# The first loads of a fused attention and feed-forward kernel, issued in another order and on other queues

## The chip, the cores and the metric

The kernel runs on one core of one Trainium2 chip. The metric is device time in microseconds (us) of the whole execution. A core has TensorE (PE in the profile; PEld is its weight load), VectorE (DVE), ScalarE (ACT), GpSimd (POOL) and SyncE (SP). SP and ACT can both issue DMA transfers; a "q" after an engine's name (SPq, ACTq) means its sequencer, which issues and waits. Times inside a profile count from the start of the span; the device time is about 1.3 us longer than the span.

The granted clock is the share of PE's full clock that the profile records. Where a trace has such records, they begin when the clock is first raised, which the mean granted clock does not count as a loss. In the profile of before the warm-up matmuls of 512 columns are 0.427 us apart. A trace that holds no clock record at all also says 1.0, so there I go by the pace of the matmuls.

## The reference, cut to what matters

```python
# x: [1, 2048, 640]; wqkv: [640, 1920]; w_phi: [32, 20, 20]; gate_w: [640]
q, k, v = split_heads(x @ wqkv)                       # 32 heads of 20
phi_k = concat(softmax(k @ w_phi), softmax(-(k @ w_phi)))    # the same for q
kv, z = phi_k.T @ v, phi_k.sum(over tokens)
a = ((phi_q @ kv) / (phi_q @ z + 1e-6)) @ wo
b = (gelu(x @ w_gate) * (x @ w_up)) @ w_down
out = sigmoid((x * gate_w).sum(-1)) * a + (1 - ...) * b
```

The tokens come in 16 tiles of 128. The change touches only the first 30 us: how x and wqkv arrive, and the first products of v.

## The kernel before

Two parts of the kernel matter. The first issues the loads. `xtok` holds the first four tiles of x in token order, and PE transposes them itself. `xT` holds x transposed; its other twelve tiles are transposed by the DMA on the way in (`dma_start_transpose`), as are wk and wq. `w3[:, kt, 0:640]` is the kt-th block of 128 rows of the v weights; I call these five loads "the rows of wv". `sc.dma(queue, ..., reads, writes)` makes the issuing engine wait for whatever the named keys need.

```python
xload("sp", 0)                      # tiles 0 and 1 of x
xload("act", 2)                     # tiles 2 and 3, beside it
sc.dma("act", ... wphi ...)
for kt in range(KD):                # KD = 5
    sc.dma("sp", ... self.w3[:, kt, 0:D] <- w3[:, kt, 2*D:3*D] ..., writes=[("wv", kt)])
sc.dma("act", ... gate row ...)
xturn(4, 2)                         # x of tiles 4 and 5, transposing load on SP
wload(self.wkT, D, "wkT")           # wk, transposing load
xturn(6, 2)
wload(self.wqT, 0, "wqT")
xturn(8, 4); xturn(12, 4)
# ... all other weights, on SP
```

The second is what TensorE does first. `vs(t, kt)` multiplies tile t by row block kt of wv. PE takes its instructions in order, so when the data of one are missing, everything behind it waits. A bank is a part of PSUM (ps in the profile), where PE's products lie until ACT or DVE evacuates them, that is, copies them out. To fold a row block of wk or wq is to multiply it by w_phi; `pq` is a product of x with the folded wq; the gram is phi_k.T @ v.

```python
warm(7)                             # 7 matmuls of zeros, to raise PE's clock
xt(0, 6, "d"); xt(1, 7, "a"); xt(2, 2, "d"); xt(3, 3, "a")  # transpose; evacuate on DVE / ACT
for kt in range(4):
    for t in range(4): vs(t, kt)    # (written out in the kernel)
self.blockdiag(); self.gate_column(6)
# ... vs(t, 4), v of tiles 4, 5; fold wk blocks 0, 1; v of tile 6; fold wk 2, 3, 4; v of tile 7;
# ... then k of tile 0, fold wq, ..., pq(0,1), pq(0,0), pq(0,3)
```

The softmax here doesn't subtract the row's maximum and nothing guards it: scores larger than these inputs give would overflow.

## Time and profile before

| | before |
|---|---|
| time, 6 runs | 288.41 us median, 287.72 to 289.37 |
| PE busy | 281.2 of 286.9 us (98%) |
| first real work on PE | 4.29 us |
| rows of wv landed | 4.96, 6.43, 6.86, 7.30, 7.80 us |
| x of tiles 6 and 7 landed | 14.76 us |
| wq landed | 19.97 us |

The landings are read from the semaphore updates in the trace. The page of the kernel before shows the busy share of each engine in its first part:

```profile
PE 281.2 (98%) x3017; PEld 185.5 (65%) x3032; DVE 174.7 (61%) x353; ACT 105.0 (37%) x199; POOL 5.3 (2%) x36
```

PE has almost no room, so a change of the loads can win or lose only where PE waits. Here is PE's timeline of the first 15 us in the kernel before. The columns are start, length, engine, line, operation, output and inputs, and count; the brackets hold idle time and who ended it.

```profile
4.29 1.29 PE L291 MATMUL ps<-ident,xtok 128*128 128x128 bf16 x20
5.42 4.72 PE L364 MATMUL ps<-w,xT 128*128 128x480 bf16 x32
9.98 0.22 PE L314 MATMUL ps<-ident,gz 128*128 128x128 bf16 x1
10.03 1.25 PE L364 MATMUL ps<-w,xT 128*128 128x480 bf16 x8
11.33 2.66 PE L352 MATMUL ps<-w,xT 128*128 128x512 bf16 x19
13.84 0.79 PE L332 MATMUL ps<-BD,wkT 128*128 128x140 bf16 x12
14.80 1.04 PE L352 MATMUL ps<-w,xT 128*128 128x512 bf16 x4 [0.18 <-DMA xT<-in_A_x_dram]
```

The 32 first v matmuls (L364) follow one another from 5.42 to 10 us. The view of waits, limited to PE and the first 30 us, lists every wait of PE above 0.15 us in the kernel before (total, times, longest):

```profile
PE ps L541 <- DVE zero L537: 1.2, 1, 1.2
PE ps L352 <- ACT Eq L519: 0.3, 1, 0.3
PE ps L352 <- DMA xT<-in_A_x_dram: 0.2, 1, 0.2
```

### The profile page before, as it was taken

To read this page: it belongs to the slowest core of one execution; us is meant where nothing else is said; L and a number is where in the kernel's file an instruction comes from. 1 tells how busy PE (TensorE), PEld (TensorE's weight loads), DVE (VectorE), ACT (ScalarE), POOL (GpSimd) and SP (SyncE) were. 2 spreads that over 40 slices of the span, in tenths; PEclk is the share of its full clock that TensorE was granted. 3 is DMA by queue.
4 is the path that set the end of the run, shared out by engine and by line. 5 is a ranking of instruction groups with operands and counts; after the bars stand their busy time and mean duration, and the time that the engine had idled before them with its cause. 6 is when DMAs were issued, how large, how long until landed. Compare 5 with 4: busy or idle time off the path is not lost.

```text
span 286.9 us, 7006 instructions
## 1 busy us (share of the span) xinstructions
PE 281.2 (98%) x3017; PEld 185.5 (65%) x3032; DVE 174.7 (61%) x353; ACT 105.0 (37%) x199; POOL 5.3 (2%) x36
## 2 busy tenths in 40 slices
PE   8999999999999999999999999999999999999996
PEld 3666689999994444444444444445777777777785
DVE  3248999999977553567242334225883883883801
ACT  3367887677663322322323223221112112112111
POOL 7000000000000000000000000000000000000000
PEclk9999999999999999999999999999999999999999
DMA  8999995000002000011000000000232333422221
GB/s 226 206 187 247 367 367 174 0 2 2 2 0 48 0 0 0 3 24 23 2 0 0 0 2 0 0 2 0 25 94 62 35 48 92 49 49 85 56 72 48
DMA packets 36937, 18.67 MB, mean 65 GB/s; under 512 B 28970, under 2 KB 36394, under 8 KB 36906
## 3 DMA queue, kind: packets, MB, share of 16 engines
q1 hardware_dynamic: 36096, 17.86, 26.1%
q8 instruction: 24, 0.39, 0.6%
q10 hardware_dynamic: 810, 0.35, 0.5%
q14 instruction: 7, 0.06, 0.1%
HBM read 9.04 MB, written 2.62 MB: 41 GB/s over the span
## 4 chain that ended last, share of the span: by engine, by line
PE 93%; SPq 3%; DMA 2%; ACT 1%; issue 1%; ACTq 0%
PE ps L352 60%; PE ps L714 28%; PE ps L658 2%; DMA xT<-in_A_x_dram 2%; PE ps L450 2%; SPq L221 2%; PE ps L332 1%; SPq L234 1%; SPq L225 1%; ACT Ek L414 0%; ACT Eq L519 0%; SPq L217 0%; ACT outsb L727 0%; ACT gcol L417 0%; ACTq L42 0%
## 5 line engine op out<-in xcount | busy, mean ns | idle before, releaser
L352 PE MATMUL ps<-xT,wg_sb 128*128 128x512 bf16 (+1 forms) x265 | 63.8, 379 | 0.4 <-issue 0.2
L352 PE MATMUL ps<-xT,wu_sb 128*128 128x512 bf16 (+1 forms) x263 | 63.3, 379 | 0.5 <-DVE hT L632 0.2
L630 ACT ACTIVATE gl<-ps 128x512 bf16<-128x512 f32 x52 | 30.9, 596 | 73.1 <-PE ps L352 68.7
L632 DVE TENSOR_TENSOR hT<-ps,gl 128x512 bf16<-128x512 f32 x39 | 26.7, 690 | 38.6 <-PE ps L352 38.5
L714 PE MATMUL ps<-wd_sb,hT 64*128 64x320 bf16 x648 | 49.5, 296 | 0.0
L352 PEld LDWEIGHTS ps<-xT,wu_sb 128*128 128x128 bf16 (+1 forms) x270 | 26.5, 99 | 29.8 <-DVE hT L632 0.5
L352 PEld LDWEIGHTS ps<-xT,wg_sb 128*128 128x128 bf16 (+1 forms) x270 | 26.2, 99 | 29.0 <-ACT gl L630 0.2
L352 PE MATMUL ps<-w,xT 128*64 128x512 bf16 (+6 forms) x398 | 41.6, 325 | 0.4 <-DMA xT<-in_A_x_dram 0.2
L727 ACT ACTIVATE outsb<-ps,Gm 128x320 bf16<-128x320 f32 (+2 forms) x31 | 14.5, 515 | 72.4 <-PE ps L714 72.4
L352 PEld LDWEIGHTS ps<-w,xT 128*64 128x64 bf16 (+1 forms) x400 | 35.8, 107 | 5.1 <-DMA xT<-in_A_x_dram 0.4
L714 PEld LDWEIGHTS ps<-wd_sb,hT 64*128 64x128 bf16 x648 | 31.0, 94 | 12.1 <-issue 0.4
L714 PE MATMUL ps<-wo_sb,goT 64*128 64x320 bf16 (+2 forms) x340 | 27.8, 288 | 0.0
L352 PE MATMUL ps<-xT,wq 128*64 128x512 bf16 (+1 forms) x184 | 26.1, 381 | 0.4 <-ACT Eq L519 0.3
L434 DVE TENSOR_TENSOR Ek<-Ek,Dk 128x640 bf16<-128x640 bf16 x32 | 25.0, 822 | 0.6
L685 DVE TENSOR_TENSOR O<-ps,RH 128x640 bf16<-128x640 f32 x32 | 24.8, 816 | 0.0
L425 DVE TENSOR_REDUCE Dk<-Ek 128x64 f32<-128x1280 bf16 x16 | 23.7, 1479 | 0.1
L519 ACT ACTIVATE Eq<-ps 128x512 bf16<-128x512 f32 x40 | 21.7, 605 | 1.1 <-PE ps L352 0.8
L414 ACT ACTIVATE Ek<-ps 128x640 bf16<-128x640 f32 x32 | 20.7, 703 | 3.6 <-PE ps L352 3.6
L632 DVE TENSOR_TENSOR xT<-ps,gl 128x512 bf16<-128x512 f32 x13 | 9.0, 691 | 18.2 <-PE ps L352 18.2
L714 PEld LDWEIGHTS ps<-wo_sb,goT 64*128 64x128 bf16 x340 | 16.1, 94 | 5.4
L352 PEld LDWEIGHTS ps<-xT,wq 128*64 128x64 bf16 (+1 forms) x185 | 15.3, 109 | 3.4 <-ACT Eq L519 0.8
L714 PE MATMUL ps<-wd_sb,xT 64*128 64x320 bf16 (+2 forms) x270 | 16.7, 269 | 0.0
(69 smaller groups left out, 173.2 us busy)
## 6 DMA issues: line engine op xcount, KB each, us to landing
out_dram<-outsb SPq DMA_DIRECT2D x7, 320.0 KB, 2.3
wd_sb<-in_B_w_down_dram SPq DMA_DIRECT2D x1, 2080.0 KB, 14.3
wg_sb<-in_B_w_gate_dram SPq DMA_DIRECT2D x1, 1120.0 KB, 5.7
wu_sb<-in_B_w_up_dram SPq DMA_DIRECT2D x1, 1120.0 KB, 8.2
wg_sb<-in_B_w_gate_dram SPq DMA_DIRECT2D x1, 960.0 KB, 9.8
wu_sb<-in_B_w_up_dram SPq DMA_DIRECT2D x1, 960.0 KB, 10.4
w<-in_A_wqkv_dram SPq DMA_DIRECT2D x5, 160.0 KB, 4.7
wo_sb<-in_A_wo_dram SPq DMA_DIRECT2D x1, 800.0 KB, 9.7
```

The costliest lines, as they stand in the source:

```text
L221: sc.dma("sp", lambda e: e.dma_start_transpose(T[:, :, :], self.wqkv[:, c0:c0 + D]), writes=[key])
L352: self.sc.op("pe", lambda e: e.matmul(self.ps[a:z, bank * 512 + c0:bank * 512 + c0 + n], lhs[:, a:z], rhs, start=first, stop=fin), reads=r ...
L414: self.sc.op("act", lambda e, s=s, scale=scale: e.activation(self.Ek[:, se, s, :], self.ps[:, o:o + self.D], AF.Exp, scale=scale), reads=[ ...
L425: sc.op("dve", lambda e: e.tensor_reduce(self.Dk[:, se, 0, :].rearrange("p (s h) -> p s h", h=H), self.Ek[:, se, :, :].rearrange("p s (h d ...
L434: sc.op("dve", lambda e, v=v, r=r: e.tensor_tensor(v, v, r, ALU.mult), reads=[("Rk", se)], writes=[("Ek", se, s)])
L450: sc.op("pe", lambda e: e.matmul(self.ps[a:a + 64, b * 512 + c:b * 512 + c + 2 * nf], va[:, lo:lo + 64], self.Ek[:, se, :, f0:f0 + nf], st ...
L519: sc.op("act", lambda e, s=s, scale=scale: e.activation(self.Eq[:, s, i, b * self.BT:(b + 1) * self.BT], self.bank(bank), AF.Exp, scale=sc ...
L630: sc.op("act", lambda e: e.activation(self.gl[:, slot, :], self.bank(banks[0]), AF.Gelu_apprx_tanh), reads=[("ps", banks[0])], writes=[("g ...
L632: sc.op("dve", lambda e: e.tensor_tensor(hT, self.bank(banks[1]), self.gl[:, slot, :], ALU.mult), reads=[("ps", banks[1]), ("gl", slot)], ...
L685: dve(lambda e, o=o, f=f, s=s: e.tensor_tensor(o, V[s][:, :, :, 0:DH], f, ALU.mult), rb + [key(6 + s)], [("O", s, sl)], guard=old)
L714: sc.op("pe", lambda e: e.matmul(self.bank(bk, w), lhs, rhs, start=opens and x == 0, stop=end and not opens, skip_group_check=True), reads ...
L727: sc.op("act", lambda e: e.activation(dst, self.bank(bk, w), AF.Copy, scale=g), reads=rd, writes=wr)
```

## The change

Its intent is to start PE's real work sooner and to remove those waits. The first two tiles of x get the DMA engines to themselves. Two of the five rows of wv go to ACT's queue, so that SP comes to its transposing loads sooner; they wait for x so as not to compete with it. w_phi and the gate row, needed late, go last. wk is turned in two parts, so that x of tiles 6 and 7 need not wait behind all of it. The warm-up reads a constant in place of a memset buffer, and pq(0,3) gets a free bank.

```diff
+        def vload(q, a, z):
+            sc.dma(q, lambda e: e.dma_start(self.w3[:, a:z, 0:D], w3[:, a:z, 2 * D:3 * D]),
+                   reads=[("xtok", 0)] if q == "act" else (), writes=[("wv", kt) for kt in range(a, z)])
...
-        xload("sp", 0)
-        xload("act", 2)
-        sc.dma("act", ... wphi ...)
+        sc.op("act", ... a first Exp, to load its table early ...)
+        for j in (0, 2):
+            xload("sp", j)
         for kt in range(KD):
-            sc.dma("sp", ... w3[:, kt, 0:D] ...)
-        sc.dma("act", ... gate row ...)
+            vload("act" if kt % 2 else "sp", kt, kt + 1)
         xturn(4, 2)
-        wload(self.wkT, D, "wkT")
+        wload(self.wkT, D, "wkT", 0, 2)
         xturn(6, 2)
-        wload(self.wqT, 0, "wqT")
+        wload(self.wkT, D, "wkT", 2, 5)
+        wload(self.wqT, 0, "wqT", 0, 5)
...
-        warm(7)
+        for n in (512, 512, 512, 512, 512, 512, 128):
+            ... matmul of the constant 1.0, n columns ...
...
-        xt(3, 3, "a")
+        xt(3, 3, "d")
+        sc.dma("act", ... wphi ...)
+        sc.dma("act", ... gate row ...)
...
-        self.pq(0, 3, 3)
+        self.pq(0, 3, 3, 0)
```

(Left out: the keys of wk and wq become one per row block, so that folding a block waits for its part only.)

More of the change, by code (lines that the diff above doesn't have):

```diff
@@ L156, in alloc @@
         self.ident = T("ident", [P, P], BF16)
-        self.zero = T("zero", [P, 512], BF16)
         self.gz = T("gz", [P, P], BF16)
@@ L218, in xload, with wload @@
                    writes=[("xtok", j), ("xtok", j + 1)])
-        def wload(T, c0, key):
-            sc.dma("sp", lambda e: e.dma_start_transpose(T[:, :, :], self.wqkv[:, c0:c0 + D]), writes=[key])
+        def vload(q, a, z):
+            sc.dma(q, lambda e: e.dma_start(self.w3[:, a:z, 0:D], w3[:, a:z, 2 * D:3 * D]),
+                   reads=[("xtok", 0)] if q == "act" else (), writes=[("wv", kt) for kt in range(a, z)])
+        def wload(T, c0, key, a, z):
+            sc.dma("sp", lambda e: e.dma_start_transpose(T[:, :, a * P:z * P], self.wqkv[a * P:z * P, c0:c0 + D]),
+                   writes=[(key, k) for k in range(a, z)])
         def xturn(t, n):
@@ L227, in loads @@
         sc.op("pool", lambda e: e.memset(self.gz[:, :], 0.0), writes=["gz"])
-        xload("sp", 0)
-        xload("act", 2)
-        sc.dma("act", lambda e: e.dma_start(
-            self.wphi_sb[:, :, :], self.wphi.rearrange("h d f -> (h d) f").rearrange("(i p) f -> p i f", p=P)),
-            writes=["wphi"])
+        sc.op("act", lambda e: e.activation(self.gtmp[:, 0:1], self.nc.const_aps.tensor(1.0, [P, 1], BF16), AF.Exp),
+              writes=["gtmp"])
+        for j in (0, 2):
+            xload("sp", j)
         for kt in range(KD):
-            sc.dma("sp", lambda e: e.dma_start(self.w3[:, kt, 0:D], w3[:, kt, 2 * D:3 * D]), writes=[("wv", kt)])
-        sc.dma("act", lambda e: e.dma_start(self.gz[0:KD, :], self.gw.rearrange("(k p) -> k p", p=P)), writes=["gz"])
+            vload("act" if kt % 2 else "sp", kt, kt + 1)
         xturn(4, 2)
-        wload(self.wkT, D, "wkT")
+        wload(self.wkT, D, "wkT", 0, 2)
         xturn(6, 2)
-        wload(self.wqT, 0, "wqT")
+        wload(self.wkT, D, "wkT", 2, 5)
+        wload(self.wqT, 0, "wqT", 0, 5)
         xturn(8, 4)
@@ L334, in fold @@
                     start=first, stop=fin, skip_group_check=True),
-                    reads=["w%sT" % which, ("BD", i)], writes=[("ps", b)], signal=fin)
+                    reads=[("w%sT" % which, kt), ("BD", i)], writes=[("ps", b)], signal=fin)
         src = self.pair(banks)
@@ L510, in kv_mask, with pq @@
                 self.kvk[i, r].append(("KV", i, r, g))
-    def pq(self, b, i, n):
+    def pq(self, b, i, n, bank=None):
         sc = self.sc
-        bank = 6 + n % 2
+        bank = 6 + n % 2 if bank is None else bank
         for kt in range(self.KD):
@@ L536, in attention_state @@
         sc = self.sc
-        sc.op("dve", lambda e: e.memset(self.zero[:, :], 0.0), writes=["zero"])
-        def warm(n):
-            for i in range(n):
-                sc.op("pe", lambda e: e.matmul(self.bank(0), self.zero[:, 0:P], self.zero[:, :], start=True, stop=True),
-                      reads=["zero"], writes=[("ps", 0)])
+        ones = self.nc.const_aps.tensor(1.0, [P, 512], BF16)
+        for n in (512, 512, 512, 512, 512, 512, 128):
+            sc.op("pe", lambda e: e.matmul(self.bank(0, n), ones[:, 0:P], ones[:, 0:n], start=True, stop=True),
+                  writes=[("ps", 0)])
         vs, ve, xt = self.v_step, self.v_first_evac, self.x_transpose
-        warm(7)
         xt(0, 6, "d")
@@ L547, in attention_state @@
         xt(2, 2, "d")
-        xt(3, 3, "a")
+        xt(3, 3, "d")
+        sc.dma("act", lambda e: e.dma_start(
+            self.wphi_sb[:, :, :], self.wphi.rearrange("h d f -> (h d) f").rearrange("(i p) f -> p i f", p=P)),
+            writes=["wphi"])
+        sc.dma("act", lambda e: e.dma_start(self.gz[0:self.KD, :], self.gw.rearrange("(k p) -> k p", p=P)), writes=["gz"])
         for t in range(4):
@@ L651, in num @@
         DB, DH = self.DB, self.DH
-        old = [("xtok", k) for k in range(4)] + ["wkT", "wqT"]
+        old = [("xtok", k) for k in range(4)] + [(w, k) for w in ("wkT", "wqT") for k in range(self.KD)]
         w = self.HB * DB
```

## The prediction

> All times are microseconds from the span's start in the profile of before, unless said otherwise.
>
> **What bounds the kernel.** TensorE. The page's first part has PE busy 281.2 of 286.9 us (98%); the chain of waits gives PE 93%, and from 30 us to the end it is PE alone but for short pieces. The change removes no matmul of that part, so all it can win is what PE loses in the first 30 us.
>
> **Where PE loses time (timeline and single instructions):**
> 1. Both x loads land together, at 4.2 and 4.4: two queues share the same engines. The Trainium skill, "DMA: Bandwidth & Descriptors", section "Issuing engines are not separate DMA queues", says DMAs interleave whoever issues them; the trace agrees: packets of both run side by side from 1.8 to 4.0. Real PE work starts at 4.28, after 7 warm-up matmuls of 0.427 us pitch that began only at 1.24, behind the memset of zero on DVE.
> 2. The first v steps wait 0.2 us for evacuations on ACT (0.70 us each, against 0.49 on DVE).
> 3. PE waits about 0.34 us before 14.80 for xT of tiles 6 and 7, queued behind the whole wkT (landing 14.75).
> 4. About 0.1 us before 20.01 for wqT (landing 19.97).
> 5. About 0.3 us before 28.34 for the Eq evacuation in the bank that pq(0,3) reuses.
>
> **What the change does.**
> - x in turn on one queue: the first half, 320 KB, should land about 3.3 (packets from 1.8 at the 300 GB/s of before, plus 0.45 us of receipt read from the trace), the second still about 4.3. Warm-up starts about 0.4 us earlier and ends about 3.5; transposes of tiles 0 and 1 then fill 3.5 to 4.3, wholly or partly at half clock. Tiles 2 and 3 follow, with DVE evacuations. I expect the first v round to end 0.3 to 0.6 us earlier (before: 6.69).
> - wv rows 1 and 3 on ACT's queue wait for x; they should land about 5.5 to 6, before they are needed. SP's queue loses two issues of 0.47 us and gains one: all transposes start about 0.45 us earlier.
> - wkT in two parts lets tiles 6 and 7 land near 12.5: loss 3 goes.
> - wphi and gate rows late: landings near 8 to 8.5, needed at about 9.6 (gate). No wait expected, margin about 1 us.
> - wqT lands about 0.45 us earlier, 19.5. PE would want it at about 19.2, so this load decides: the gain here is about 0.45, not PE's 0.8.
> - pq(0,3) into bank 0 removes loss 5: another 0.3 us.
> After that PE has hardly a wait. DVE's k_norm chain runs without a break from 25.3 to 79 but shifts too, so the gain should survive.
>
> **Predicted:** 287.75 us, 0.8 less than 288.56 (0.3%), range 286.9 to 288.6. Chances: faster by over 2% 0.01, within 2% 0.98, slower by over 2% 0.01.
>
> **What would show it right:** first transposes on PE near 3.5; no idle on PE before the matmuls that read tile 6; no wait for ACT before pq(0,3); wqT landing near 19.5 and ending a wait on PE.
>
> **What would make it wrong:** the clock released later than the 4.3 us of before, so that the early work runs at half rate (the Trainium skill, "TensorE: Matmul & The Clock Gate", Part 1: the window runs free; 0.427 us per 512 columns shows the half rate here); wphi or gate row landing after 9.6, stalling PE; split transposes taking longer in sum, delaying wqT.

## The result, and the profile after

The changed kernel took 292.96 us in the median of 6 runs, 292.49 to 293.94 in its five fast ones. The sixth, 334.62 us, ran at 0.85 of PE's clock for nearly the whole span and is set aside; no other run did that. The ratio of the changed kernel's fast runs to those of before is 1.0159 (95% interval 1.0133 to 1.0186). Ratios here are the mean time of one kernel's fast runs over that of the other's in the same rounds, so they are not quite the ratio of the medians. The kernel became 4.6 us slower (mean of the fast runs, 293.03 against 288.44) where I had forecast 0.8 us faster.

The profile taken with that result was the slow run, so I ran the same kernel again. That run (called e0_again below) is the profile after. PE is busy as long as before, in a longer span:

```profile
PE 281.1 (97%) x3017; PEld 185.8 (64%) x3032; DVE 174.9 (61%) x353; ACT 104.5 (36%) x199; POOL 5.3 (2%) x36
```

The timeline of PE in this run, from the transposes of x (L294) on:

```profile
3.76 1.71 PE L294 MATMUL ps<-ident,xtok 128*128 128x128 bf16 x20
5.66 1.25 PE L367 MATMUL ps<-w,xT 128*128 128x480 bf16 x8 [0.19 <-DMA w<-in_A_wqkv_dram]
9.74 3.45 PE L367 MATMUL ps<-w,xT 128*128 128x480 bf16 x24 [2.84 <-DMA w<-in_A_wqkv_dram]
13.04 0.22 PE L317 MATMUL ps<-ident,gz 128*128 128x128 bf16 x1
```

PE does begin 0.5 us sooner, as intended. But after the first 8 v matmuls it stands still until 9.74 us. The waits of PE over the first 30 us in this run:

```profile
PE ps L367 <- DMA w<-in_A_wqkv_dram: 3.0, 2, 2.8
PE ps L542 <- PEq L834: 0.8, 1, 0.8
```

The three small waits of before are gone or shorter, and one of 3 us is new. The chain of waits of this run, in order of time, says which DMA it was:

```profile
3.73 5.96 DMA w<-in_A_wqkv_dram
9.70 0.05 issue
9.74 3.45 PE ps L367 x24
```

The load issued at 3.73 us is row block 1 of wv, the first of the two on ACT's queue. It took 5.96 us for 160 KB. The list of DMA issues shows the two queues side by side (last column: median us from issue to landing). Before:

```profile
w<-in_A_wqkv_dram SPq DMA_DIRECT2D x5, 160.0 KB, 4.7
```

and in the run after:

```profile
w<-in_A_wqkv_dram SPq DMA_DIRECT2D x3, 160.0 KB, 3.8
w<-in_A_wqkv_dram ACTq DMA_DIRECT2D x2, 160.0 KB, 6.1
```

So the three on SP came faster than before and the two on ACT much later than was needed: row blocks 1 and 3 landed at 9.70 and 10.35 us, while PE wanted block 1 at about 6.7.

That is a pause of 3 us; the kernel lost 4.6. A second loss shows in the granted clock, which is listed for each run. Here are all fast runs of the changed kernel, from both rounds of measurement, in order of clock:

| mean granted clock | times (us) |
|---|---|
| 1.0 | 289.92 |
| 0.994 | 291.87, 292.49, 292.81, 292.85, 293.07 |
| 0.988 | 293.34, 293.73, 293.94 |

One window of 3.413 us at half clock in 291.6 us gives 1 - 0.5 * 3.413 / 291.6 = 0.994, and two give 0.988. The medians of the rows are 289.92, 292.81 and 293.73 us, so 3.8 us lie between no window and two. The steps are uneven, 2.9 us for the first window and 0.9 for the second, and the first row is a single run, so this table does not give the price of one window. By arithmetic, a window of 3.413 us at half clock that PE could fill would cost 1.7 us.

### The profile page after: what moved, and what is told of

Same layout as the page of the kernel before. It is cut to its first block, busy times and chain, and to the rows that moved or that the text cites. A ratio compares the mean times of both kernels' runs of the same rounds, so it can differ in the third digit from the quotient of the medians.

```text
span 333.3 us, 7008 instructions
## 1 busy us (share of the span) xinstructions
PE 324.9 (97%) x3017; PEld 201.5 (60%) x3032; DVE 175.9 (53%) x353; ACT 105.6 (32%) x199; POOL 5.3 (2%) x36
## 4 chain that ended last, share of the span: by engine, by line
PE 94%; DMA 3%; DVE 1%; issue 0%; ACT 0%
PE ps L355 60%; PE ps L718 28%; DMA w<-in_A_wqkv_dram 2%; PE ps L662 2%; PE ps L367 2%; PE ps L453 2%; PE ps L335 1%; DMA xtok<-in_A_x_dram 1%; DVE O L689 0%; DVE hT L636 0%; DVE RH L678 0%; ACT outsb L731 0%; DVE RH L683 0%; DVE RH L684 0%; DVE RH L682 0%
## 5 line engine op out<-in xcount | busy, mean ns | idle before, releaser
L355 PE MATMUL ps<-xT,wg_sb 128*128 128x512 bf16 (+1 forms) x265 | 73.1, 422 | 0.5 <-issue 0.2
L355 PE MATMUL ps<-xT,wu_sb 128*128 128x512 bf16 (+1 forms) x263 | 72.7, 423 | 0.6
L718 PE MATMUL ps<-wd_sb,hT 64*128 64x320 bf16 x648 | 56.4, 324 | 0.0
L355 PEld LDWEIGHTS ps<-xT,wu_sb 128*128 128x128 bf16 (+1 forms) x270 | 28.6, 107 | 36.7
L355 PE MATMUL ps<-w,xT 128*64 128x512 bf16 (+6 forms) x398 | 48.1, 359 | 0.2
L355 PEld LDWEIGHTS ps<-w,xT 128*64 128x64 bf16 (+1 forms) x400 | 38.1, 116 | 8.9
L718 PEld LDWEIGHTS ps<-wd_sb,hT 64*128 64x128 bf16 x648 | 33.6, 101 | 16.1 <-issue 0.5
L718 PE MATMUL ps<-wo_sb,goT 64*128 64x320 bf16 (+2 forms) x340 | 31.3, 315 | 0.0
L355 PE MATMUL ps<-xT,wq 128*64 128x512 bf16 (+1 forms) x184 | 30.0, 420 | 0.1
L678 DVE RECIPROCAL RH<-ps 128x32 f32<-128x32 f32 x16 | 5.7, 358 | 25.6 <-PE ps L662 25.0
## 6 DMA issues: line engine op xcount, KB each, us to landing
wo_sb<-in_A_wo_dram SPq DMA_DIRECT2D x1, 800.0 KB, 10.4
```

The source lines that it names most:

```text
L355: self.sc.op("pe", lambda e: e.matmul(self.ps[a:z, bank * 512 + c0:bank * 512 + c0 + n], lhs[:, a:z], rhs, start=first, stop=fin), reads=r ...
L718: sc.op("pe", lambda e: e.matmul(self.bank(bk, w), lhs, rhs, start=opens and x == 0, stop=end and not opens, skip_group_check=True), reads ...
```

## The experiments

All runs gave correct results except one. My theory after reading the result (M): the two rows of wv on ACT's queue were issued when the transposing loads on SP's queue began, and ordinary loads beside transposing ones crawl; PE's pause then costs clock as well. Its rivals: the wait for x made the rows late whatever ran beside them (W); two queues for wv are slow as such (Q); any backlog on SP's queue would do it (B); the loss is elsewhere, in the late w_phi or in wk in parts.

### e0_again: the changed kernel once more

No edit.

> The changed kernel once more, unedited, because its profile fell in the slow state. All theories: 292.5 to 294 us in the fast state. The trace should show the rows of wv of kt 1 landing about 10 us after the span's start, PE without work for about 3.6 us before them, and one window of 3.4 us at half clock after that, then full clock.

Measured: 292.60 us median of 4 fast runs, 289.92 to 293.73; ratio 1.0133 (1.0078 to 1.0188). Row block 1 landed at 9.7 us, as expected; PE lost 3.0 us where I had expected 3.6, and two of the four times lie below the 292.5 to 294 that I gave. The profiled run kept its full clock after the pause, which I had not expected; it is also the fastest. (Its trace has no clock record, but its 24 v matmuls after the pause took 3.45 us, against 4.93 in m2_rows_in_pieces, mostly at half clock.)

### e1_rows_on_sp: all rows of wv on SP's queue

```diff
-            vload("act" if kt % 2 else "sp", kt, kt + 1)
+            vload("sp", kt, kt + 1)
```

> One edit to the changed kernel: all five rows of wv on SP's queue, ahead of the first transposing load. Theory M (ordinary rows on the second queue that share the DMA engines with transposing loads crawl, and they do so because they were issued after x): rows land by 7.5 us, the stall of 3.6 us and the half-clock window go, 287.5 to 289 us; the late w_phi and gate rows still share with the transposes, so they may land at 9 to 10 us and cost up to 1 us at the gate column. Rival B (the time is lost elsewhere, in w_phi and gate rows last or wk in parts): stays above 291 us.

Measured: 287.88 us, 287.67 to 287.92, ratio 0.9981 (0.9967 to 0.9996). This one edit undoes the loss, and the rest of the change is then worth 0.55 us (0.1 to 0.95). So nothing else in the change costs 4 us. (Where the 0.55 us comes from is not settled by the traces; see the table of milestones below.) PE's waits in this run:

```profile
PE ps L335 <- DMA wkT<-in_A_wqkv_dram: 1.0, 1, 1.0
PE ps L542 <- PEq L834: 0.8, 1, 0.8
PE ps L294 <- DMA xtok<-in_A_x_dram: 0.3, 1, 0.3
```

The wait of 1.0 us is for the second part of wk, which now comes behind x of tiles 6 and 7 (landed at 13.4 us; the part of wk at 16.8). The late w_phi landed at 9.4 us and the gate row at 9.7, without a wait of PE.

### e2_no_wait_for_x: the two rows issued at once

```diff
-                   reads=[("xtok", 0)] if q == "act" else (), writes=[("wv", kt) ...
+                   reads=(), writes=[("wv", kt) ...
```

> One edit to the changed kernel: ScalarE's two rows of wv no longer wait for x, so they are issued at about 0.8 and 1.3 us, before any transposing load is there. Theory M: they land by about 5 us, no stall, full clock from 4.3 us on, 287.5 to 289 us, with x half a us later than in the changed kernel. Rival Q (two queues for wv as such are slow): rows still land late, above 291 us.

Measured: 289.53 us, 287.44 to 290.03, ratio 1.0016 (0.9976 to 1.0055). The rows on ACT's queue landed at 4.9 and 6.1 us:

```profile
w<-in_A_wqkv_dram ACTq DMA_DIRECT2D x2, 160.0 KB, 4.5
```

Two queues as such are not slow, so Q falls. Of the times, three lie above the 287.5 to 289 that I gave and one just below. x landed at 4.7 and 5.9 us instead of 3.7 and 4.5 in e0_again, PE stood idle for 1.1 us after the warm-up, and in the profiled run the clock was first granted in full only at 10.2 us after the span's start, against 4.3 in the profile of before.

```profile
PE ps L294 <- DMA xtok<-in_A_x_dram: 1.1, 1, 1.1
```

One run, 287.44, was faster than every run of before in the same rounds. So in this trace x did come later without the wait, as the wait was meant to prevent; that the late clock follows from it was not tested.

### e3_turn_waits_for_rows: the same two rows at the same time, without transposes beside them

```diff
-        xturn(4, 2)
+        xturn(4, 2, [("wv", 1), ("wv", 3)])     # waits until both have landed
```

> One edit to the changed kernel: the first transposing load waits until both of ScalarE's rows of wv have landed; those rows still wait for x and are issued at the same 3.7 us. Theory M: with no transposing load beside them the rows land within 2.5 us of issue, at about 5.8 to 6.3 us instead of 10.4, no stall, and the transposes, started 3 us later, still end about where they did; 287.3 to 289 us. Rival W (it is the wait for x that makes the rows late, not the company): they land near 10 us again, and the transposes start after that, so 293 us or more.

Measured: 289.80 us, 289.25 to 289.94, ratio 1.0046 (1.0031 to 1.0061). In the list of DMA issues of this run, the two rows, still issued at 3.76 us:

```profile
w<-in_A_wqkv_dram ACTq DMA_DIRECT2D x2, 160.0 KB, 3.4
```

They landed at 7.16 and 7.59 us, 2.5 and 2.8 us sooner than beside the transposes, so W falls as the main cause. It is not wholly false: M had given 5.8 to 6.3, and even so the first came about 0.5 us after PE wanted it. My time for this run was too low, because the transposes, held until 7.67 us, did not catch up:

```profile
PE ps L355 <- DMA xT<-in_A_x_dram: 1.6, 2, 1.0
PE ps L542 <- PEq L834: 0.8, 1, 0.8
PE ps L335 <- DMA wkT<-in_A_wqkv_dram: 0.6, 1, 0.6
```

The stall moved from the rows to the transposed tiles.

### m1_plain_loads: plain loads of the same bytes in place of the transposing ones

This gives wrong results (relative error 1.18): the data lie untransposed.

```diff
-   e.dma_start_transpose(self.xT[:, :, a:z], self.x[a:z, :])          # the same for wk and wq
+   for k in range(t, t + n):
+       e.dma_start(self.xT[:, :, k*P:k*P+P], self.x[k*P:k*P+P, :].rearrange("p (c t) -> p c t", t=P))
```

> Wrong results on purpose. The changed kernel with every transposing load of the input x and of wk and wq replaced by plain loads of the same bytes in pieces of 256 bytes to the same tiles, on the same queue at the same place, one for each 128 rows. Theory M (what makes ScalarE's rows of wv crawl is the transposing load beside them): the rows land at 5.5 to 7.5 us, about as in the run where the transposes waited (7.2 and 7.6), and their 1280-byte packets take about 55 to 75 ns. Rival B (any backlog of small packets on SP's queue does it): they land at 9 us or later, packets above 100 ns.

Measured: the rows landed at 8.1 and 8.8 us, between what the two theories gave, and their packets took 62 ns in the mean, as M gave. The two times, of no use as results, are 287.82 and 288.20 us. PE waited 0.9 us:

```profile
PE ps L368 <- DMA w<-in_A_wqkv_dram: 0.9, 1, 0.9
```

The packets of the trace tell the same. The table counts the 256 packets of 1280 bytes of the two rows, and the packets of 256 bytes on SP's queue (transposing ones but in m1) that began between 6 and 10 us:

| run | beside the rows on ACT's queue | mean ns of a row's packet | rows landed at | 256-byte packets on SP's queue, 6 to 10 us |
|---|---|---|---|---|
| e2_no_wait_for_x | x and other rows | 59 | 4.9, 6.1 | 2978 |
| e3_turn_waits_for_rows | other rows | 66 | 7.2, 7.6 | 593 (held) |
| m1_plain_loads | plain 256-byte pieces | 62 | 8.1, 8.8 | 2342 |
| e4_filler | transposing loads | 104 | 10.9, 11.4 | 1082 |
| e0_again | transposing loads | 116 | 9.7, 10.4 | 1357 |
| e1_rows_on_sp | no such rows | - | - | 2609 |

Both sides suffer beside one another: a row's packet takes almost twice as long, and the transposing packets come at about half the rate of e1_rows_on_sp, where all five rows went ahead of them on one queue. The longer packets are only part of the delay: 256 packets on 16 engines are 16 for each, so 50 ns more for each packet make 0.8 us (an estimate from the table); in e0_again the first of them also began 1.5 us later than in e3_turn_waits_for_rows (6.74 against 5.21). Taken from one trace of each run, the lateness has three parts, which can be read off the landings of row block 1: about 0.5 us after PE's wish with only other rows in flight (7.2 against 6.7), 0.9 us more beside plain small packets (8.1), and 1.6 to 2.8 us more because the company transposes (9.7 to 10.9). B is true of the second part, M of the largest. (m1_plain_loads also cuts each load into one for each 128 rows; that this plays no part was not tested.)

### m2_rows_in_pieces: the rows in 256-byte pieces

```diff
+            if q == "act":   # two loads for each 128 rows: column blocks 0, 2, 4 and 1, 3, in runs of 256 bytes
```

> The changed kernel with ScalarE's rows of wv in pieces of 256 bytes (two loads for each 128 rows) in place of 1280. If the crawl is a cost per packet that takes turns with a transposing one, five times the packets make it worse: rows land after 13 us. If it follows bytes or large packets, they land no later than before, 9 to 11 us. Plain issue alone: about 1 us later than before at most.

Measured: 290.28 and 291.27 us. Row block 1 was whole at 9.6 us and block 3 at 11.5. Block 3 was later than the 9 to 11 us that I gave for a cost by bytes, but five times the packets did not bring the 13 us and more of a cost for each packet, so a fixed cost for each packet that takes its turn is not the main cause. This run also caught the half clock in its profile. Two windows of 3.41 us each, with the granted clock after the engines' busy times:

```profile
5.97:9.38 3.41, 1.47 (x11) 0.60 (x9) 0.74 (x2) 0.70 (x1) 1.11 (x8) 1.00 1.31 183
9.38:12.79 3.41, 3.10 (x12) 1.61 (x13) 0.00 (x0) 0.00 (x0) 0.00 (x0) 0.50 1.25 219
```

PE was busy for 1.47 of 3.41 us in the first window; the second window ran at 0.50 of the clock, and PE, though busy, got 12 matmuls done in it. In the same run the 24 v matmuls took 4.93 us in the timeline, against 3.45 in e0_again:

```profile
9.70 4.93 PE L373 MATMUL ps<-w,xT 128*128 128x480 bf16 x24 [1.71 <-DMA w<-in_A_wqkv_dram]
```

The trace of the changed kernel's slow run, at 0.85 of the clock elsewhere, has such a pair too:

```profile
7.97:11.38 3.41, 0.93 (x7) 0.57 (x8) 0.00 (x0) 0.00 (x0) 0.00 (x0) 0.85 1.22 181
11.38:14.79 3.41, 3.41 (x15) 1.78 (x14) 1.19 (x5) 0.00 (x0) 0.00 (x0) 0.50 1.01 204
```

In e0_again the pitch of the transposes falls from 107 to 56 ns at 4.69 us, so the clock became full there. If windows of 3.41 us follow one another from that point, the pause falls across two of them:

```profile
4.69:8.11 3.42, 2.03 (x21) 1.23 (x19) 1.20 (x3) 0.70 (x1) 2.17 (x13) 1.00 1.15 235
8.11:11.52 3.41, 1.78 (x13) 1.12 (x14) 0.64 (x3) 0.00 (x0) 0.00 (x0) 1.00 1.26 192
```

So the windows with PE busy for 1.47 and 0.93 us were followed by half clock, and these with 2.03 and 1.78 were not. Nor was one with 1.85 in e3_turn_waits_for_rows (15.54 to 18.95 us, the windows counted from its first record of full clock at 5.30). This would explain why the same pause lowered the clock in 8 runs of 9 and not in this one: it depends on how the pause falls across the windows. It is a reading of four traces and was not tested; why some runs lost two windows is open.

### e4_filler: PE kept busy during the stall

```diff
         for t in range(4):
             vs(t, 0)
+        for n in range(13):
+            ... matmul of the constant 1.0, 512 columns, into a bank that is free then ...
```

> The changed kernel with 13 matmuls of constants (512 columns, 2.8 us in all at full clock) put where PE stands still for the row of wv of kt 1; they go to a PSUM bank that nothing else uses then. Theory C (the changed kernel loses more than the stall itself, because the pause of PE sends its clock back to half for one or two windows of 3.4 us, about 1.8 us each): the mean granted clock is 1.0 in every run and the time 289.5 to 290.5 us, the same as the one run of the changed kernel that kept its clock (289.92). Rival N (the low clock has nothing to do with the pause): clock 0.988 to 0.994 in most runs and 292 to 294 us as before.

Measured: 290.93 us, 289.79 to 291.20, ratio 1.0090 (1.0072 to 1.0108), and the clock is 1.0 in all 6 runs. The changed kernel's nine fast runs include only one with 1.0. By the ratios to before, thirteen useless matmuls make the kernel 2.0 us faster than in the first measurement and 1.2 us faster than in e0_again:

```profile
6.73 3.00 PE L556 MATMUL ps<-const-bfloat16-1.0 128*128 128x512 bf16 x13
10.93 1.27 PE L367 MATMUL ps<-w,xT 128*128 128x480 bf16 x8 [1.20 <-DMA w<-in_A_wqkv_dram]
```

The stall itself remains, here until 10.93 us, which is why the median lies above the 290.5 I allowed. So the pause of PE, not something else in the change, lowers the clock. (The changed kernel was not run on the chip of e4_filler; before had 1.0 there in all 11 runs.)

### e5_small_early: all rows on SP, and w_phi and the gate row at the start

```diff
-            vload("act" if kt % 2 else "sp", kt, kt + 1)
+            vload("sp", kt, kt + 1)
-        sc.dma("act", ... wphi ...); sc.dma("act", ... gate row ...)      # after the transposes of x
+        sc.dma("act", ... wphi ...); sc.dma("act", ... gate row ...)      # right after the loads of x
```

> All rows of wv on SP (as in the first edit), and w_phi and gate rows issued at the start on ScalarE's queue, as the kernel before does. Theory M: no ordinary load runs beside the transposes any more, so the first transposing load lands about 0.5 us earlier than 9.9 us, and the second part of wk about as much earlier than 16.8 us, for which PE waited 1.1 us: 287.2 to 287.6 us, against 287.88 with the small loads late. If late small loads cost nothing: 287.8 to 288.2 us (x 0.2 us later).

Measured: 287.37 us, 287.20 to 287.56, ratio 0.9971 (0.9954 to 0.9987). The first transposing load landed at 8.85 us in place of 9.90, and the second part of wk at 16.3 in place of 16.8, for which PE waited 0.4 us instead of 1.0. Again on another chip (e5_again): 287.95 us, ratio 0.9974 (0.9959 to 0.9990), above the 287.2 to 287.6 that I gave first.

> The changed kernel with all rows of wv on SP and the small loads early, again, for a comparison on one chip: 287.2 to 287.6 us; if chips or launches differ in the phase of the clock's window, up to 288.3 us.

### e6_wk_whole: all rows on SP, wk in one load

```diff
-        wload(self.wkT, D, "wkT", 0, 2)
+        wload(self.wkT, D, "wkT", 0, 5)
         xturn(6, 2)
-        wload(self.wkT, D, "wkT", 2, 5)
```

> All rows of wv on SP, and wk transposed in one load as in the kernel before (tiles 4 and 5, wk, tiles 6 and 7, wq). Theory S (each transposing load has a slow tail, so the split of wk costs about 1 us of DMA time): wq lands near 19.5 us instead of 20.4, PE waits 0.3 to 0.6 us for tiles 6 and 7 instead of 1.1 us for wk's second part: 287.3 to 287.6 us. If the split is good as intended: 288.0 us or more.

Measured: 289.06 us, 288.35 to 290.25, ratio 1.0036 (1.0015 to 1.0057). wq landed at 19.7 us against 20.4 with the split, which theory S had right, but tiles 6 and 7 landed at 15.8 us, and PE waited 0.9 us for them instead of the 0.3 to 0.6 I gave. One run, 290.25 us, shows 0.994 of the clock, though the profiled run has no pause above 0.9 us; that run has no trace, so what PE did in it is open. The split of wk is good in this setting, as the change intended, and my theory of its cost led to the wrong sign.

### e7_bank_only: the kernel before with pq(0,3) in another bank

```diff
-        self.pq(0, 3, 3)
+        self.pq(0, 3, 3, 0)
```

> The kernel before with one edit: pq(0,3) into bank 0. The prediction said 0.3 us from this alone: 288.1 us where before is 288.4. If the wait only moves to the next evacuation: no difference, within 0.1 us.

Measured: 288.04 us against 288.33, ratio 0.9995 (0.9977 to 1.0013). The wait of 0.3 us for ACT's Eq is no longer among PE's waits in this run, but in the time the gain can't be told from nothing. The trace tells it apart: the stretch from the first pq to the first gram takes 3.18 us instead of 3.62 (see the milestones). In the profiled run the first v matmul began at 6.07 us, against 5.42. The pitch of the transposes shows why: here 12 of the 19 steps from one to the next take 93 to 107 ns, in before all but the first take 55 to 57. So the clock became full about 1.3 us later in this run. Differences of this size between runs hide the gain.

### e8_x_in_turn_only: the kernel before with both loads of x on SP

```diff
-        xload("act", 2)
+        xload("sp", 2)
```

> The kernel before with one edit: the second load of x on SP's queue behind the first, instead of ScalarE's beside it. The prediction's first step: x lands at 3.3 and 4.3 us, but the warm-up (still behind the memset of zero) ends at 4.2 and the transposing loads are issued 0.47 us later, so little is left: 288.0 to 288.6 us, no difference from before.

Measured: 289.04 us, 288.14 to 289.63, ratio 1.0019 (1.0001 to 1.0037): if anything slower. SP issues one load more ahead of its transposing loads. The first of them was issued 0.48 us later than before (4.09 against 3.62 us), x of tiles 6 and 7 landed at 16.5 us instead of 14.8, and PE waited for it:

```profile
PE ps L352 <- DMA xT<-in_A_x_dram: 1.2, 1, 1.2
```

Half a microsecond of issue does not explain 1.7 us of landing; what else delayed that load is open. The clock of this trace was also full only from 5.92 us, against 4.30.

### b1, b2, b3: x of tiles 4 to 7 ahead of all of wk

These three mend the order as well: e5_small_early, with x of tiles 4 to 7 transposed before wk, and PE taking v of tile 6 before it folds wk. b1 loads the four tiles in one transposing load, b2 in two; b3 is b2 with 8 full warm-up matmuls.

```diff
-        wload(self.wkT, D, "wkT", 0, 2)
         xturn(6, 2)
-        wload(self.wkT, D, "wkT", 2, 5)
+        wload(self.wkT, D, "wkT", 0, 5)
...
+        self.v_early(6, 6)
         f(0, "k", (2, 3), "d")
         f(1, "k", (4, 5), "a")
-        self.v_early(6, 6)
         ...    # f(2) to f(4) and v of tile 7 into other banks
```

> All rows of wv on SP, w_phi and gate rows early, and x of tiles 4 to 7 transposed in one load ahead of wk in one load; TensorE projects v of tile 6 before it folds wk. Theory S (each transposing load ends in a slow tail of about 1 us): tiles 4 to 7 land by 10.5 us, wk by 14.3, wq by 18.8, PE waits for none of them: 286.6 to 287.0 us. If there is no such tail: tiles 4 and 5 come late with tiles 6 and 7, PE waits about 0.5 us for them, 287.2 us or more.

> The same with x of tiles 4 and 5 and of 6 and 7 in a load each. Theory S: 1 us more DMA time before wk than with one load, wk lands near 15 us, PE waits up to 0.3 us for it: 286.8 to 287.3 us. Without a tail: the same as or better than one load.

> The reordered kernel with x of tiles 4 to 7 in two loads, with 8 full warm-up matmuls in place of 6 and a quarter, so that PE has no pause before the transposes of x. Theory P (a pause of PE in the first 4 us delays the release of the clock in some runs): all runs within 0.3 us of each other, at 287.0 to 287.4 us. If pauses don't matter: two groups again, 287.2 and 288.3 us.

> The reordered kernel with two loads again, for a comparison on one chip: 287.1 to 288.3 us in two groups, as before.

Measured: b1 287.98 us (ratio 0.9984, 0.9966 to 1.0002), b2 287.80 (0.9981, 0.9964 to 0.9998), b2 again 287.72 (0.9967, 0.9952 to 0.9982), b3 287.96 (0.9976, 0.9960 to 0.9991). In b2's second profile PE has no wait above 0.2 us for any load:

```profile
PE ps L545 <- PEq L833: 0.8, 1, 0.8
PE ps L297 <- DMA xtok<-in_A_x_dram: 0.2, 1, 0.2
```

Still it is not faster than e5_small_early beyond the noise. The longer warm-up did not narrow the spread (287.44 to 288.25), so my theory P is not confirmed. The mended versions lie 0.2 to 0.3% below before in the same rounds, with intervals that exclude equality for e5 (both times), b2 (both times) and b3, and I can't rank them.

### Milestones of PE, read from the traces

When PE started certain work (us from the span's start), in the profiled run of each kernel:

| run | first transpose | first v | v, block 1 | gate | first fold of wq | first pq | first gram | last matmul | span |
|---|---|---|---|---|---|---|---|---|---|
| before | 4.29 | 5.42 | 6.69 | 9.98 | 20.01 | 25.90 | 29.52 | 283.88 | 286.94 |
| e7_bank_only | 4.33 | 6.07 | 7.32 | 10.60 | 20.20 | 26.09 | 29.27 | 283.59 | 286.24 |
| e8_x_in_turn_only | 4.21 | 6.15 | 7.39 | 10.68 | 21.68 | 27.34 | 31.18 | 285.51 | 288.39 |
| e0_again | 3.76 | 5.66 | 9.74 | 13.04 | 22.62 | 28.50 | 31.70 | 286.02 | 288.68 |
| e1_rows_on_sp | 4.00 | 5.42 | 6.57 | 9.85 | 20.49 | 26.37 | 29.56 | 283.89 | 286.62 |
| e5_small_early | 3.82 | 5.52 | 6.67 | 9.96 | 20.00 | 25.88 | 29.07 | 283.37 | 286.31 |
| b2_x_first_two_loads | 3.84 | 5.53 | 6.68 | 9.96 | 19.69 | 25.35 | 28.76 | 283.08 | 285.89 |

Three things are to be read here. From the first gram to the last matmul takes 254.3 to 254.4 us in every row, so all is decided in the first 30 us and nothing is given back later. From the first pq to the first gram takes 3.62 us in before and 3.84 in e8_x_in_turn_only, which keep the old bank, and 3.18 to 3.20 in e7, e0, e1 and e5 with the new one: this one-word edit is worth about 0.4 us. (b2 and the other runs on its chip or on that of e5_again take 3.40 to 3.41 with the new bank; e8, with the old bank on the chip of b2, takes 3.84, so there it is 0.4 us again.) And at the first fold of wq, e5_small_early is where before was, at 20.00 us: the new order of loads has gained nothing there. e1_rows_on_sp has no lead over before at the first gram either; in this pair of traces its lead of 0.3 us lies behind the last matmul.

## Why the prediction was wrong

Point by point, as the prediction put it:

- "wv rows 1 and 3 on ACT's queue wait for x; they should land about 5.5 to 6, before they are needed." This is the step that failed. They landed at 9.7 and 10.4 us, and PE waited 3.0 us. I had costed them as an ordinary load after an ordinary load and had looked only at when SP's transposes would be issued, not at what would then run beside ACT's rows. e1_rows_on_sp shows that the loss goes with this choice (the converse, the kernel before with only these two rows moved, was not run); e2_no_wait_for_x, e3_turn_waits_for_rows and m1_plain_loads show, in one trace each, that the queue is innocent and that the company of transposing loads is the largest part.
- The clock. I named a late first release as a risk, but in e0_again it came at 4.7 us, against 4.3. I had no term for a second fall of the clock. The pause of 3 us cost one or two windows of half clock in 8 of the 9 fast runs. e4_filler, which keeps PE busy, had 1.0 in 6 of 6.
- The sum. e1_rows_on_sp gives -0.55 us for the rest of the change. The ratio of e4_filler gives +2.6 us over before with the stall but without the clock, so the stall would be worth about 3.1 us. The changed kernel's +4.6 (first measurement) or +3.8 us (e0_again, with one run at full clock) leaves 2.0 or 1.2 us for the clock. The split is not firm: row block 1 landed 1.2 us later in e4_filler's trace than in e0_again's, and the one run of the changed kernel at full clock is only 1.5 us above before (289.92 against 288.43), which leaves 3.1 or 2.3. A pause of 3 us also need not cost 3: e0_again is 3.2 us behind e1_rows_on_sp at the gate and 2.1 at the first fold of wq, since e1_rows_on_sp waits 1.0 us for wk between them. So the clock is worth 1 to 3 us.
- "I expect the first v round to end 0.3 to 0.6 us earlier" did not hold either. PE began on x earlier, at 3.76 to 4.00 us (predicted 3.5), but began row block 1 at 6.57 and 6.67 us in e1_rows_on_sp and e5_small_early, which have no stall, against 6.69 before. The first half of x landed sooner, at 3.7 us in e0_again against 4.2, but the second half at 4.5 (e0_again) to 4.9 us (e5_small_early) against 4.4, and row block 0 of wv at 5.2 to 5.5 us against 4.96. What the first load of x won, the next loads on the queue lost, and PE needs both.
- "wqT lands about 0.45 us earlier ... the gain here is about 0.45" failed as well: the first fold of wq began at 20.00 us in e5_small_early and 20.49 in e1_rows_on_sp, against 20.01. The new wait for wk's second part took the place of the one for tiles 6 and 7.
- "wkT in two parts lets tiles 6 and 7 land near 12.5: loss 3 goes." They landed at 13.0 (e5_small_early) and 13.4 us (e1_rows_on_sp), and PE's wait for them went. I had missed that PE then waits for the second part of wk, 0.4 to 1.0 us.
- "No wait expected" for w_phi and gate row, landing near 8 to 8.5. They landed at 10.9 us in e0_again, under cover of the stall, and at 9.4 and 9.7 us in e1_rows_on_sp, just in time.
- "pq(0,3) into bank 0 removes loss 5: another 0.3 us" was right and a little low: 0.4 us in the milestones. In the time of e7_bank_only it can't be told from nothing.
- The size of the gain, 0.8 us, is about what the mended e5_small_early reaches: 287.37 and 287.95 us on two chips, 0.26 to 0.29% below before. But the milestones put about 0.4 us of it on the bank alone, so it does not rescue the prediction's account of the loads.

What stays open: why an ordinary and a transposing load slow each other. m2_rows_in_pieces speaks against a cost for each packet's turn; the small w_phi packets of 40 bytes took 12 ns beside transposing loads in e1_rows_on_sp and 11 without, but 15 in e4_filler, and the 256-byte pieces of m2_rows_in_pieces took 25.5 ns on ACT's queue, where m1_plain_loads has 19 on SP's. Why tiles 6 and 7 came so late in e8_x_in_turn_only, and the run at 0.85 of the clock are open too. For the runs of one kernel that differ by half a microsecond the traces hold a candidate that was not tested: the moment when the clock first becomes full, 3.49 us in b2_x_first_two_loads (287.14 us) and 6.41 in b2_again (287.72).

The Trainium skill helps here only in part. "DMA: Bandwidth & Descriptors", section "Rules for kernel authors", says that spreading DMAs over issuing engines does not help bandwidth and "only saves sequencer issue time". The runs agree where ordinary loads share (e2_no_wait_for_x: 59 ns a packet on ACT's queue, 57 on SP's) and go beyond it where transposing loads share: there the spreading cost 3 us. "TensorE: Matmul & The Clock Gate", Part 1, gives the window as 3413 ns and the low clock as one half; the trace of m2_rows_in_pieces has 3.413 us at 0.50.

## What to carry to other kernels

When a load is moved to a second queue to save issue time, ask what will be in flight on the first queue while it lands; beside a transposing load, an ordinary one took nearly twice as long for each packet here, and the transposes slowed as well. Put the ordinary loads that the matrix engine needs first ahead of the transposing ones on one queue, or issue them so early that they have landed. Count a pause of the matrix engine of about 3 us as more than its length: here it took one or two windows of half clock with it in 8 runs of 9, and harmless matmuls in the gap bought 1.2 to 2.0 us back.

## What the Trainium skill lacked or had wrong

- "DMA: Bandwidth & Descriptors", section "Rules for kernel authors", says of correctness that "A transpose next to ordinary DMAs needs nothing". All such runs were correct, so that holds; but the page lacks the cost: packets of 1280 bytes took 104 to 116 ns in the mean beside transposing loads on the other queue, 59 to 66 ns beside ordinary ones, and the transposing packets between 6 and 10 us were 1357 instead of 2609.
- "TensorE: Matmul & The Clock Gate", section "HAM oscillation", gives the rule as no idle gap of PE longer than about 3.4 us. In m2_rows_in_pieces no pause before the fall was longer than 1.7 us, and the clock still fell to 0.50 for one window, after a window in which PE was busy for 1.47 of 3.41 us. In e0_again's profiled run, a pause of 2.8 us was followed by matmuls at full pace. The busy share of a window (0.93 and 1.47 us before a fall, 1.78 to 2.03 without one), not the length of one gap, agrees with the traces, but four traces don't prove that.
- No page gives the time from issue to landing of a small transposing load. "DMA: Bandwidth & Descriptors" has a bandwidth (section "Latency and other measured facts", 261 GB/s). In e3_turn_waits_for_rows the first one, 320 KB, was issued at 7.67 us, when the last ordinary load of the first stage, w_phi, had 0.2 us left to land, and landed at 12.1 us.
